# A linear-attention and rational-MLP kernel on one core: a new order of the steps behind step 107

## The chip, the core and the metric

One core of a Trainium2 chip. The metric is the device time of one execution in microseconds (us). Five instruction streams run beside each other and wait for one another through semaphores: PE (TensorE), DVE (VectorE), ACT (ScalarE), POOL (GpSimd) and SP (SyncE, here only an issuer of DMAs). Each works through its own instructions strictly in the order in which they were written.

## The reference

Gated linear attention over 4 batches, 8 heads, 768 positions and 48 channels, followed by a two-layer MLP with a rational activation on all 3072 tokens:

```
f = sigmoid(f_logit)                                   # per batch, head, position, channel
state_t = f_t * state_(t-1) + k_t v_t^T                # 48x48 per head
y_t = q_t state_t                                      # 8 heads x 48 = 384 per token
h = y @ w_in                                           # 384 -> 2048
P = a0 + a1 h + a2 h^2 + a3 h^3
Q = 1 + |b0| |h| + |b1| h^2
out = (P / (Q + 1e-6)) @ w_out                         # 2048 -> 384
```

## The kernel before

The tokens are cut into 12 units of 256 tokens: unit n is chunk n // 4 of batch n % 4, so four units of one chunk are independent and unit n needs the state that unit n - 4 left. Everything that a unit needs is cut into small steps, and one long string, `ORDER` (line 19), names all 823 steps of the 12 units in the order in which they are recorded. A step is a function of the same name (table `steps`, line 587); it writes one instruction or several dozen, all on one engine. `ORDER` therefore fixes the order of every engine's instructions and of every DMA queue. No scheduler moves anything afterwards; semaphores only make an instruction wait until its inputs are there and its buffer is free. The first number of a step is its unit, the last two, where there are any, the blocks of 128 hidden channels (0 to 16) that it covers, and `@s` names one of four PSUM slots that a tile takes.

The steps that the text below speaks of:

- loads: `ld n f|k|q` on SP, `ld n v` on POOL (both line 193); `wi`, `wo` load the weights on POOL (lines 199, 205).
- attention: `ef`, `ls` (ACT, sigmoid in logs), `cs` (PE, prefix sums), `A` (ACT, exponentials), `xa n 0|1` (DVE, scaled q and k, line 308), `T` (PE transposes), `Te` (ACT copy), `sc` (PE scores), `mk` (DVE mask, line 353), `vm n 0|1` (POOL, two small copies of V columns, line 360), `yb`, `yi` (PE, outputs, line 367), `kv`, `si` (PE), `ae` (ACT) and `st` (DVE, line 445) for the state, `ye` (ACT copy to `xT`).
- MLP: `h` (PE, 12 matmuls for 4 blocks, line 454), `hy` (ACT cast to bf16, line 484), `sq` = h^2 (DVE, line 489), `ab` = |h| (DVE, line 497), `p1`, `pm`, `p2` (DVE, lines 531, 545, 536) for P; the sum that ends P is made either by DVE (`tv`, line 553) or by an accumulating DMA that POOL issues (`ta`, line 549); likewise the sum in Q by DVE (`zv`, line 515), by a POOL DMA (`zd`, line 519) or on PE (`u`, line 505). `lz` or `ln` takes the logarithm of Q (ACT, lines 523, 510), `ex` its negative exponential (ACT, line 527), `gm` multiplies (DVE, line 557), `o` is the second matmul (PE, line 567), `oe` the copy out (line 574), `so` the store. `dz` is a dummy matmul (line 295).

The V columns of a unit go to one of two buffers, `vmp0` for even units and `vmp1` for odd ones. Two of the steps on POOL, one DVE step and the loop that records the steps read:

```python
def vm(n, x):
    s = unit(n)
    vv = s["v"].rearrange("p (a r) i d -> p r i a d", r=2)
    src = vv[:, 0, :, :, 32:48] if x == 0 else vv[:, 1, :, :, 0:16]
    nc.gpsimd.tensor_copy(s["vm"][:, :, :, 32 * x:32 * x + 16], src)
def ta(n, m0, m1):
    nc.gpsimd.dma_start(out=fl(s["g"], m0, m1), in_=fl(s["hy"], m0, m1), accum_op=ALU.add)
def gm(n, m0, m1):
    return nc.vector.tensor_mul(fl(s["g"], m0, m1), fl(s["g"], m0, m1), fl(qi, m0, m1))
for step in ORDER.replace("\n", ";").split(";"):
    name, *args = step.split()
    marks[...] = steps[name](...)
```

Of the kernel before, what the change touches and what calls it, by code (L numbers as in the profile page):

```python
# [32 lines left out]
u 0 8 12 @3; A 3 0; ta 0 8 16; sq 0 0 4; Te 2 s; h 1 0 4 @2; vm 2 1; xa 3 0; wo 8 12; ln 0 8 12; p2 0 0 8
sc 2 0 @0; kv 2 @1; ef 5; mk 2 0; si 2 0; ae 2; hy 1 0 4; sc 2 1 @3; st 2 0; yb 2 0 2 @0; ex 0 8 16; mk 2 1
si 2 1; u 0 0 4 @2; ab 1 0 8; u 0 4 8 @3; ln 0 0 4; st 2 1; p1 1 0 16; u 1 12 16 @1; ln 0 4 8; yi 2 1; sq 1 0 8
ln 1 12 16; yb 2 2 4; kv 3 @3; ye 2 s; pm 1 8 16; T 3 @2; ae 3; ef 4; si 3 0; h 2 0 4 @0; p2 1 0 16; Te 3 s
ls 4; st 3 0; u 1 8 12 @1; ta 1 8 16; pm 0 0 8; hy 2 0 4; ld 7 f; si 3 1; wo 12 16; dz 1 @2; h 2 8 12 @2
ln 1 8 12; st 3 1; ld 5 v; pm 1 0 8; ex 0 0 8; vm 4 1; sc 3 1 @0; sc 3 0 @3; mk 3 1; h 2 4 8 @1; vm 3 1; wo 4 8
hy 2 8 12; wo 0 4; mk 3 0; cs 4 @0; ls 5; vm 4 0; h 2 12 16 @2; vm 3 0; tv 0 0 8; A 4 0; ld 8 f; ld 5 q; A 4 1
xa 4 0; yi 3 1 @3; ld 6 k; yb 3 0 2; hy 2 4 8; ld 6 q; u 1 4 8 @0; xa 4 1; hy 2 12 16; yb 3 2 4; gm 0 8 16  # L40
cs 5 @1; ld 6 v; ye 3 s; T 4 @2; gm 0 0 8; A 5 0; ln 1 4 8; h 3 0 4 @3; p1 2 0 16; Te 4 s; h 3 12 16 @0
ab 2 0 16; hy 3 0 4; o 0 1 8 12 @2; tv 1 0 8; A 5 1; kv 4 @3; hy 3 12 16; sq 2 0 16; u 1 0 4 @1; ae 4; ex 1 8 16
o 0 0 8 12; si 4 0; o 0 1 12 16; xa 5 1; vm 5 1; ln 1 0 4; h 3 8 12 @0; zd 2 8 16; p2 2 0 16; ld 8 k; ef 6
h 3 4 8 @1; ef 7; pm 2 0 16; hy 3 8 12; o 0 1 4 8; hy 3 4 8; sc 4 1 @0; o 0 1 0 4; ls 6; mk 4 1; ta 2 8 16
sc 4 0 @1; ex 1 0 8; o 0 0 0 4; ld 9 f; xa 5 0; cs 6 @0; mk 4 0; o 0 0 4 8; A 6 1; o 0 0 12 16; st 4 0; A 6 0
yb 4 0 2 @1; ab 3 0 16; yb 4 2 4; oe 0 0 2 s; yi 4 0; yi 4 1; si 4 1; sq 3 0 16; ye 4 s; T 5 @2; ef 8
u 2 0 4 @1; Te 5 s; h 4 4 8 @0; st 4 1; zd 3 8 16; ln 2 0 4; gm 1 8 16; h 4 12 16 @2; lz 2 8 16; p1 3 0 16
# [578 lines left out]
```

## Time and profile before

| | us |
|---|---|
| median of 3 runs | 217.37 (215.85 to 218.01) |
| span of the profiled execution, first to last instruction | 214.4 |
| PE busy | 201.0 (94%) |
| DVE busy | 201.7 (94%) |
| ACT busy | 195.8 (91%) |
| POOL busy | 83.7 (39%) |

The span is the only time that the profile gives for the profiled execution; it lies 3.0 us below the median of the runs and 1.45 us below the lowest. What is predicted is the time of such a run. Busy time is time with an instruction in work; DMA issues on POOL count, on SP they don't. Times inside the trace are counted from the start of the span.

### The profile page before, as it was taken

What the parts mean: (1) busy time and instruction counts of PE and PEld (TensorE: products, weight loads), DVE (VectorE), ACT (ScalarE), POOL (GpSimd) and SP (SyncE); (2) the same over time, 40 slices, a digit from 0 to 9 for tenths busy, and PEclk for the clock granted to TensorE, in tenths of its full rate; (3) what the DMA queues carried; (4) which work ended last, traced back from release to release, by engine and by line L of the source; (5) the groups of instructions that cost most, each with busy time, mean ns of one, the idle gap of its engine ahead of it and who ended that gap; (6) DMA issues with size and microseconds to landing.
All of it is one profiled execution on the core that took longest, in us unless ns stands there. A gap on an engine that the chain in (4) does not pass through costs nothing.

```text
span 214.4 us, 7128 instructions
## 1 busy us (share of the span) xinstructions
PE 201.0 (94%) x3166; PEld 139.9 (65%) x3166; DVE 201.7 (94%) x213; ACT 195.8 (91%) x204; POOL 83.7 (39%) x93
## 2 busy tenths in 40 slices
PE   5875999899999999999999899999999999999993
PEld 1544587567767686586687587686577676776461
DVE  4786899999999999999999999999999999999991
ACT  3574689999999999999999999999999999999990
POOL 5161009009165072183270496696350603114200
PEclk9999999999999999999999999999999999999999
DMA  5999999999999999999999499999499896988823
GB/s 143 240 257 217 201 242 197 195 223 223 187 200 248 247 235 219 253 228 203 192 292 193 81 294 215 209 225 208 89 192 200 164 196 126 174 282 151 187 84 148
DMA packets 61199, 43.20 MB, mean 202 GB/s; under 512 B 51184, under 2 KB 55024, under 8 KB 61168
## 3 DMA queue, kind: packets, MB, share of 16 engines
q0 software_dynamic: 21520, 23.86, 67.3%
q1 hardware_dynamic: 39360, 18.68, 34.5%
q8 instruction: 25, 0.41, 0.8%
q10 hardware_dynamic: 288, 0.20, 0.3%
q14 instruction: 6, 0.05, 0.1%
HBM read 25.17 MB, written 4.72 MB: 139 GB/s over the span
## 4 chain that ended last, share of the span: by engine, by line
PE 39%; DVE 29%; ACT 14%; DMA 9%; issue 6%; SPq 2%; POOL 1%; DVEq 0%
PE hp L454 13%; PE op L567 12%; DVE gall L557 6%; DMA w_in_sb<-in_moe_w_in_dram 6%; DVE gall L545 4%; ACT qi L527 4%; ACT hy L484 4%; DVE z L497 3%; DVE h L489 3%; DVE scm L353 3%; DMA fn<-in_f_logit_dram 3%; PE u L505 3%; DVE gall L531 3%; PE y L367 2%; DVE hy L536 2%
## 5 line engine op out<-in xcount | busy, mean ns | idle before, releaser
L567 PE MATMUL op<-w_out_sb,gall 128*128 128x384 bf16 x384 | 69.2, 326 | 0.4 <-DVE gall L557 0.4
L454 PE MATMUL hp<-xT,w_in_sb 128*128 128x256 bf16 x564 | 66.7, 273 | 2.1 <-DMA w_in_sb<-in_moe_w_in_dram 2.0
L454 PEld LDWEIGHTS <-w_in_sb 128*128 128x128 bf16 x564 | 54.2, 98 | 11.5 <-DMA w_in_sb<-in_moe_w_in_dram 2.5
L567 PEld LDWEIGHTS <-gall 128*128 128x128 bf16 x384 | 36.1, 98 | 23.6 <-DVE gall L557 0.8
L484 ACT CAST hy<-hp 128x1024 bf16<-128x1024 f32 x47 | 48.1, 1076 | 2.3 <-PE hp L478 1.4
L527 ACT ACTIVATE qi<-lq 128x2048 bf16<-128x2048 f32 (+1 forms) x26 | 48.0, 1861 | 0.1
L360 POOL COPY vmp<-vn 128x128 bf16<-128x128 bf16 x24 | 35.2, 1516 | 28.4 <-DMA vn<-in_v_dram 22.7
L549 POOL DMA_DIRECT2D gall<-hy x20 | 20.0, 1068 | 53.9 <-ACT lsp L276 10.6
L523 ACT ACTIVATE lq<-z 128x2048 f32<-128x2048 bf16 (+1 forms) x20 | 36.8, 1874 | 0.0
L353 DVE TENSOR_TENSOR scm<-sc,mask 128x1024 bf16<-128x1024 f32 x24 | 29.0, 1215 | 1.9 <-PE sc L345 1.7
L489 DVE TENSOR_TENSOR h<-hy 128x4096 bf16<-128x4096 bf16 (+2 forms) x19 | 28.5, 1500 | 0.0
L557 DVE TENSOR_TENSOR gall<-gall,qi 128x4096 bf16<-128x4096 bf16 (+2 forms) x17 | 28.2, 1666 | 0.2
L545 DVE TENSOR_TENSOR gall<-gall,h 128x4096 bf16<-128x4096 bf16 (+2 forms) x17 | 28.1, 1652 | 0.0
L519 POOL DMA_DIRECT2D z<-h x17 | 19.3, 1366 | 17.0 <-PE u L505 6.0
L302 ACT ACTIVATE A<-cs 128x768 f32<-128x768 f32 (+1 forms) x26 | 19.4, 799 | 1.8 <-PE cs L286 1.8
L193 POOL DMA_DIRECT2D vn<-in_v_dram x12 | 12.4, 1030 | 15.7 <-PE y L367 7.9
L531 DVE TENSOR_SCALAR gall<-hy,a_sb 128x4096 bf16<-128x4096 bf16 (+1 forms) x14 | 16.9, 1208 | 0.0
L536 DVE TENSOR_SCALAR hy<-hy,a_sb 128x4096 bf16<-128x4096 bf16 (+1 forms) x14 | 16.6, 1185 | 0.0
L497 DVE TENSOR_SCALAR z<-hy 128x4096 uint16<-128x4096 uint16 (+2 forms) x19 | 15.7, 834 | 0.4 <-ACT hy L484 0.4
L330 ACT COPY qkT<-tp 128x1024 f32<-128x1024 f32 x11 | 11.6, 1058 | 3.2 <-PE tp L320 3.2
L320 PE MATMUL tp<-ident,qkp 128*128 128x128 bf16 x192 | 12.9, 219 | 0.8 <-DVE qkp L308 0.5
L320 PEld LDWEIGHTS <-qkp 128*128 128x128 bf16 x192 | 11.5, 98 | 2.5 <-DVE qkp L308 0.9
(73 smaller groups left out, 255.8 us busy)
## 6 DMA issues: line engine op xcount, KB each, us to landing
gall<-hy POOLq DMA_DIRECT2D x18, 512.0 KB, 7.1
z<-h POOLq DMA_DIRECT2D x15, 512.0 KB, 8.4
fn<-in_f_logit_dram SPq DMA_DIRECT2D x11, 384.0 KB, 8.5
kn<-in_k_dram SPq DMA_DIRECT2D x11, 384.0 KB, 12.1
qn<-in_q_dram SPq DMA_DIRECT2D x11, 384.0 KB, 11.3
out_dram<-osb SPq DMA_DIRECT2D x11, 384.0 KB, 5.1
vn<-in_v_dram POOLq DMA_DIRECT2D x12, 192.0 KB, 8.9
w_in_sb<-in_moe_w_in_dram POOLq DMA_DIRECT2D x4, 384.0 KB, 10.1
```

Of the source, the lines that this page charges most:

```text
L320: nc.tensor.transpose(t[:, x, i, p, :], s["qk"][:, i, x, 2 * p:2 * p + 2, :].rearrange("t h d -> t (h d)"), ident)
L353: return nc.vector.tensor_mul(t, s["sc", g].rearrange("s r a i t -> s (r a) (i t)"), mb)
L360: nc.gpsimd.tensor_copy(s["vm"][:, :, :, 32 * x:32 * x + 16], src)
L454: nc.tensor.matmul(t[:, m - m0, :], w_in_sb[:, kk, m * P:(m + 1) * P], s["x"][:, kk].rearrange("p i j t -> p (i j t)"), start=(kk == 0), s ...
L484: (nc.scalar.copy if eng == "s" else nc.vector.tensor_copy)(fl(big(s, "hy", "hy", 3), m0, m1), fl(s["hp", m0], 0, m1 - m0))
L489: return nc.vector.tensor_mul(fl(big(s, "h2", "h2", 2), m0, m1), fl(s["hy"], m0, m1), fl(s["hy"], m0, m1))
L523: nc.scalar.activation(fl(lq, m0, m1), fl(s["z"], m0, m1), AF.Ln, scale=regs[2], bias=1.0 + 1e-6)
L527: nc.scalar.activation(fl(qi, m0, m1), fl(lq, m0, m1), AF.Exp, scale=-1.0)
L531: return nc.vector.tensor_scalar(fl(big(s, "g", "gall", 3), m0, m1), fl(s["hy"], m0, m1), a_sb[:, 3:4], a_sb[:, 2:3], op0=ALU.mult, op1=AL ...
L545: return nc.vector.tensor_mul(fl(s["g"], m0, m1), fl(s["g"], m0, m1), fl(s["h2"], m0, m1))
L557: return nc.vector.tensor_mul(fl(s["g"], m0, m1), fl(s["g"], m0, m1), fl(qi, m0, m1))
L567: nc.tensor.matmul(s["op", j][:, j, 0:DM], s["g"][:, m, P * j:P * j + P], w_out_sb[:, m, :], start=(s["on", j] == 1), stop=(s["on", j] == KF))
```

## The change

Only the string `ORDER` changes. Its first 107 steps (up to `A 2 0`) stay as they are. Behind them stand the same 716 steps, each as often as before and with the same arguments, in another order, and some of their PSUM tiles take another of the four slots. No function, shape, buffer or step is added or removed. The changed kernel is one line shorter, so every line number in it is one lower.

```diff
-yb 1 0 2 @1; st 1 0; yb 1 2 4; sq 0 12 16; yi 1 1; si 1 1; p1 0 8 16; ye 1 s; h 0 4 8 @2; ab 0 12 16; ef 3
+yb 1 0 2 @0; vm 2 0; yb 1 2 4; ef 3; st 1 0; sq 0 12 16; p1 0 8 16; yi 1 1; si 1 1; vm 2 1; ye 1 s; h 0 4 8 @1
...
```

Three places show what that does to the queues. On DVE, first, the stretch from the second half of unit 0's P to the first mask of unit 2 (`h2`, which the profile calls `h`, is made by `sq`, `z` by `ab`, `gall` by `p1` and `pm`, `hy` by `p2`, `qkp` by `xa`, `scm` by `mk`); tiles with 467 are unit 0's `hy`, those with 721 or 723 unit 1's. Before:

```order
L536 TENSOR_SCALAR hy_467<-hy_467,a_sb_104 128x2048
L497 TENSOR_SCALAR z_472<-hy_467 128x1024
L489 TENSOR_TENSOR h2_532<-hy_467 128x1024
L308 TENSOR_TENSOR qkp0_87<-kn_326,A_89 128x2x8x48
L497 TENSOR_SCALAR z_740<-hy_721 128x2048
L489 TENSOR_TENSOR h2_760<-hy_721 128x2048
L497 TENSOR_SCALAR z_472<-hy_467 128x1024
L308 TENSOR_TENSOR qkp0_87<-qn_336,A_89 128x2x8x48
L531 TENSOR_SCALAR gall_671<-hy_467,a_sb_104 128x2048
L308 TENSOR_TENSOR qkp1_88<-kn_338,A_89 128x2x8x48
L489 TENSOR_TENSOR h2_532<-hy_467 128x1024
```

and with the change:

```order
L488 TENSOR_TENSOR h2_532<-hy_467 128x1024
L535 TENSOR_SCALAR hy_467<-hy_467,a_sb_104 128x2048
L496 TENSOR_SCALAR z_472<-hy_467 128x1024
L307 TENSOR_TENSOR qkp0_87<-kn_326,A_89 128x2x8x48
L496 TENSOR_SCALAR z_760<-hy_723 128x2048
L488 TENSOR_TENSOR h2_762<-hy_723 128x2048
L307 TENSOR_TENSOR qkp0_87<-qn_336,A_89 128x2x8x48
L488 TENSOR_TENSOR h2_532<-hy_467 128x1024
L530 TENSOR_SCALAR gall_660<-hy_467,a_sb_104 128x2048
L307 TENSOR_TENSOR qkp1_88<-kn_338,A_89 128x2x8x48
L496 TENSOR_SCALAR z_472<-hy_467 128x1024
```

The square `sq 0 4 8` now stands ahead of `p2 0 8 16`, and `ab 0 0 4` and `sq 0 0 4` have changed places across three other steps.

On POOL, second, the same time: the copies `vm` (`vmp<-vn`), the V loads (`vn`; 445 is unit 2's), the weight loads and the first accumulating DMA, `ta 0 8 16` (`gall<-hy_467`). Before:

```order
L360 COPY vmp0_94<-vn_445 128x8x16
L193 DMA vn_779<-in_v_dram 128x8x96
L193 DMA vn_800<-in_v_dram 128x8x96
L549 DMA gall_671<-hy_467 128x2048
L360 COPY vmp0_94<-vn_445 128x8x16
L205 DMA w_out_sb_111<-in_moe_w_out_dram 128x4x384
L549 DMA gall_964<-hy_721 128x2048
```

and with the change, where `vn_791` is unit 3's V and `vn_904` unit 4's:

```order
L359 COPY vmp0_94<-vn_445 128x8x16 x2
L192 DMA vn_791<-in_v_dram 128x8x96
L192 DMA vn_904<-in_v_dram 128x8x96
L204 DMA w_out_sb_111<-in_moe_w_out_dram 128x4x384
L359 COPY vmp0_94<-vn_904 128x8x16
L359 COPY vmp1_95<-vn_791 128x8x16
L548 DMA gall_660<-hy_467 128x2048
```

`ta 0 8 16` has moved behind the copies `vm 4 0` and `vm 3 0`, which read the two V tiles whose loads are issued just ahead.

On POOL, third, the middle of the program: `z` is written by `zd`, `gall` by `ta`. Before (unit 7's V is `vn_1762`; `z_1985` and `gall_2007` are unit 4's):

```order
L360 COPY vmp1_95<-vn_1762 128x8x16
L549 DMA gall_1705<-hy_1371 128x2048
L519 DMA z_1985<-h2_1897 128x2048
L193 DMA vn_2138<-in_v_dram 128x8x96
L193 DMA vn_2322<-in_v_dram 128x8x96
L360 COPY vmp1_95<-vn_1762 128x8x16
L519 DMA z_2243<-h2_2283 128x2048
L549 DMA gall_2007<-hy_1738 128x2048
```

and with the change (unit 8's V is `vn_1832`, unit 7's `vn_2061`; `z_1968` and `gall_2083` are unit 4's):

```order
L192 DMA vn_2061<-in_v_dram 128x8x96
L359 COPY vmp0_94<-vn_1832 128x8x16
L518 DMA z_1968<-h2_1850 128x2048
L359 COPY vmp1_95<-vn_2061 128x8x16
L548 DMA gall_2083<-hy_1704 128x2048
```

`zd 4 8 16` now stands behind the copy `vm 8 1`, which may overwrite `vmp0` only when `yb 6` has read it, and `ta 4 0 8` behind `vm 7 1`.

More of the change, by code (lines that the diff above doesn't have):

```diff
@@ L33 @@
[L33 to L47, printed above, removed]
@@ new lines @@
+h 1 12 16 @0; ls 3; pm 0 8 16; ab 0 12 16; st 1 1; hy 0 4 8; h 1 8 12 @2; sq 0 4 8; hy 1 12 16; hy 1 8 12
+cs 3 @3; p2 0 8 16; ab 0 4 8; h 0 0 4 @0; xa 2 1; h 1 4 8 @2; ab 1 8 16; sq 1 8 16; A 3 1; hy 0 0 4; xa 2 0
+u 0 12 16 @0; T 2 @1; hy 1 4 8; A 3 0; ld 3 v; u 0 8 12 @2; sq 0 0 4; ln 0 12 16; Te 2 s; p1 0 0 8; xa 3 1
+ab 0 0 4; h 1 0 4 @3; sc 2 0 @0; ln 0 8 12; xa 3 0; p2 0 0 8; hy 1 0 4; kv 2 @1; si 2 0; dz 1 @2; sc 2 1 @3
+mk 2 0; ae 2; ld 4 v; st 2 0; mk 2 1; ex 0 8 16; yb 2 0 2 @0; si 2 1; st 2 1; u 0 0 4 @2; ef 5; ln 0 0 4
@@ new lines @@
+ef 7; sc 4 0 @1; mk 4 0; cs 6 @0; o 0 0 8 12; o 0 0 4 8; xa 5 0; yi 4 1 @1; yi 4 0; yb 4 0 2; ld 7 k; A 6 1
+yb 4 2 4; oe 0 0 2 s; si 4 1; T 5 @2; A 6 0; ab 3 0 16; sq 3 0 16; ye 4 s; ta 2 0 8; st 4 1; u 2 0 4 @1
+h 4 4 8 @0; lz 2 8 16; p1 3 0 16; gm 1 8 16; gm 1 0 8; Te 5 s; h 4 0 4 @3; hy 4 4 8; ln 2 0 4; h 4 12 16 @2
+ef 8; h 4 8 12 @0; sc 5 0 @1; pm 3 0 16; hy 4 12 16; zd 3 8 16; hy 4 0 4; u 2 4 8 @2; ta 2 8 16; hy 4 8 12
+sc 5 1 @3; mk 5 0; ex 2 8 16; kv 5 @0; ld 6 v; si 5 0; zd 3 0 8; ae 5; vm 5 1; mk 5 1; ld 8 v; o 1 1 12 16 @1
@@ new lines @@
+pm 4 0 16; o 2 1 8 12; p2 4 0 16; o 2 1 4 8; o 2 0 4 8; o 2 1 12 16; st 6 0; ld 10 f; ld 8 k; ex 3 0 8; mk 6 0
+xa 7 1; hy 5 12 16; ex 3 8 16; o 2 1 0 4; yi 6 0 @0; yi 6 1; ls 8; T 7 @1; so 0 0 2 s; lz 4 0 8; o 2 0 8 12
+si 6 1; Te 7 s; tv 4 8 16; sq 5 0 16; yb 6 0 2; yb 6 2 4; ye 6 s; o 2 0 0 4; ab 5 0 16; oe 2 0 2 s; vm 8 1
+cs 8 @1; ld 8 q; st 6 1; h 6 0 4 @0; ld 11 f; ld 9 k; zd 4 8 16; vm 7 1; ta 4 0 8; A 8 0; A 8 1; vm 7 0
+sc 7 1 @2; gm 3 0 16; h 6 4 8 @3; hy 6 0 4; ef 10; ld 9 q; h 6 12 16 @0; o 3 1 12 16 @1; vm 8 0; so 2 0 2 s
@@ new lines @@
+mk 7 1; p1 5 0 16; sc 7 0 @2; zd 5 0 8; hy 6 4 8; kv 7 @3; ex 4 0 8; xa 8 1; hy 6 12 16; si 7 0; o 3 1 8 12
+zv 5 8 16; o 3 1 0 4; ae 7; ld 9 v; ld 10 q; mk 7 0; h 6 8 12 @0; yb 7 2 4 @2; yb 7 0 2; lz 4 8 16; st 7 0
+yi 7 1; si 7 1; p2 5 0 16; xa 8 0; ls 9; hy 6 8 12; pm 5 0 16; o 3 0 8 12; ta 5 8 16; ld 10 v; o 3 0 12 16
+cs 9 @0; yi 7 0; st 7 1; o 3 0 0 4; ex 4 8 16; gm 4 0 16; A 9 1; ye 7 s; o 3 0 4 8; o 3 1 4 8; A 9 0; lz 5 8 16
+ab 6 0 16; sq 6 0 16; h 7 8 12 @3; h 7 4 8 @0; oe 3 0 2 s; kv 8 @2; hy 7 8 12; ef 11; si 8 0; T 8 @1; ae 8
@@ new lines @@
+hy 7 4 8; xa 9 1; Te 8 s; h 7 0 4 @3; hy 7 0 4; st 8 0; sc 8 0 @2; kv 9 @0; p1 6 0 16; ld 10 k; vm 9 0; ta 5 0 8
+zd 6 8 16; sc 8 1 @3; zd 6 0 8; vm 9 1; o 4 1 8 12 @1; o 4 0 12 16; mk 8 0; mk 8 1; si 9 0; o 4 0 8 12
+h 7 12 16 @2; ls 10; ex 5 8 16; lz 5 0 8; pm 6 0 16; yi 8 0 @3; yb 8 0 2; ae 9; st 9 0; yb 8 2 4; o 4 0 4 8
+vm 10 1; yi 8 1; o 4 1 4 8; xa 9 0; p2 6 0 16; ls 11; hy 7 12 16; ex 5 0 8; o 4 1 12 16; cs 10 @0; ye 8 s
+o 4 0 0 4; o 4 1 0 4; T 9 @2; h 8 0 4 @3; A 10 0; A 10 1; oe 4 0 2 s; h 8 8 12 @1; sq 7 0 16; lz 6 8 16
@@ new lines @@
+o 5 1 4 8; o 5 0 8 12; si 10 0; dz 3 @2; h 9 0 4 @2; p1 8 0 16; h 9 8 12 @3; lz 7 0 8; ta 7 0 8; ae 10; st 10 0
+oe 5 0 2 s; p2 8 0 16; ex 7 0 8; zd 8 8 16; hy 9 0 4; hy 9 8 12; lz 7 8 16; h 9 4 8 @1; xa 11 1; xa 11 0
+sc 10 1 @2; sc 10 0 @0; h 9 12 16 @3; hy 9 12 16; hy 9 4 8; mk 10 1; ex 7 8 16; mk 10 0; o 6 1 8 12 @2
+o 6 1 4 8; o 6 1 12 16; T 11 @0; yi 10 0 @3; yi 10 1; ta 7 8 16; yb 10 2 4; yb 10 0 2; Te 11 s; so 3 0 2 s
+o 6 0 8 12; pm 8 0 16; o 6 0 4 8; ab 9 0 16; sc 11 0 @1; sq 9 0 16; mk 11 0; o 6 0 0 4; o 6 0 12 16; ta 8 8 16
@@ new lines @@
+o 6 1 0 4; ye 10 s; lz 8 0 8; lz 8 8 16; h 10 0 4 @1; gm 7 0 16; oe 6 0 2 s; h 10 8 12 @3; ta 8 0 8; hy 10 0 4
+sc 11 1 @2; h 10 12 16 @1; p1 9 0 16; ex 8 0 8; kv 11 @0; hy 10 8 12; ex 8 8 16; mk 11 1; ae 11; p2 9 0 16
+o 7 0 4 8 @2; pm 9 0 16; hy 10 12 16; o 7 1 8 12; h 10 4 8 @3; si 11 0; o 7 0 8 12; gm 8 0 16; zd 9 0 8
+hy 10 4 8; o 7 1 0 4; o 7 1 4 8; yi 11 0 @3; lz 9 0 8; st 11 0; so 1 0 2 s; o 7 0 12 16; yi 11 1; yb 11 0 2
+yb 11 2 4; sq 10 0 16; zd 9 8 16; o 7 1 12 16; o 7 0 0 4; lz 9 8 16; ab 10 0 16; p1 10 0 16; zv 10 0 8; ye 11 s
@@ new lines @@
+h 11 8 12 @1; o 8 0 8 12 @0; ex 9 0 8; hy 11 8 12; oe 7 0 2 s; ta 9 8 16; ex 9 8 16; o 8 0 4 8; ta 9 0 8
+o 8 0 12 16; p2 10 0 16; o 8 1 0 4; h 11 0 4 @3; h 11 12 16 @2; zd 10 8 16; o 8 0 0 4; pm 10 0 16; o 8 1 12 16
+o 8 1 4 8; o 8 1 8 12; ab 11 8 12; gm 9 0 16; sq 11 8 12; lz 10 0 8; so 7 0 2 s; lz 10 8 16; hy 11 12 16
+o 9 1 12 16 @1; h 11 4 8 @2; ex 10 8 16; ex 10 0 8; tv 10 8 16; p1 11 8 16; oe 8 0 2 s; o 9 0 0 4; o 9 1 0 4
+sq 11 12 16; ab 11 12 16; pm 11 8 12; o 9 1 8 12; o 9 0 8 12; o 9 1 4 8; ta 10 0 8; p2 11 8 16; gm 10 0 16
@@ new lines @@
+pm 11 12 16; so 6 0 2 s; hy 11 0 4; o 9 0 4 8; o 9 0 12 16; so 8 0 2 s; zd 11 8 12; hy 11 4 8; lz 11 8 12
+sq 11 0 4; sq 11 4 8; ab 11 4 8; ab 11 0 4; o 10 0 0 4 @0; oe 9 0 2 s; o 10 0 12 16; so 9 0 2 s; o 10 1 12 16
+zd 11 12 16; ta 11 8 12; o 10 1 8 12; p1 11 0 8; lz 11 12 16; ex 11 8 12; o 10 0 8 12; ex 11 12 16; so 5 0 2 s
+u 11 4 8 @1; ln 11 4 8; p2 11 0 8; ta 11 12 16; zv 11 0 4; ex 11 4 8; lz 11 0 4; pm 11 0 4; o 10 1 0 4
+o 10 1 4 8; o 10 0 4 8; ex 11 0 4; gm 11 12 16; o 11 0 12 16 @1; pm 11 4 8; gm 11 8 12; o 11 1 12 16 @3
@@ L98 @@
+o 11 0 8 12; oe 10 0 2 s; so 10 0 2 s; tv 11 4 8; o 11 1 8 12; gm 11 4 8; o 11 0 4 8; o 11 1 4 8; tv 11 0 4
+gm 11 0 4; o 11 1 0 4; o 11 0 0 4; dz 1 @2; oe 11 0 1 v; oe 11 1 2 s; so 11 0 1 s; so 11 1 2 a
 """
```

73 lines of the change are left out of this document (20 added, 53 removed).

## The prediction

> **What bounds the kernel now.** I read the page first, for which engine is full, then the table of windows, for where it is full, then the waits, and last the chain of waits, for what sets the end.
>
> ```profile
> span 214.4 us, 7128 instructions
> PE 201.0 (94%) x3166; PEld 139.9 (65%) x3166; DVE 201.7 (94%) x213; ACT 195.8 (91%) x204; POOL 83.7 (39%) x93
> DVE  4786899999999999999999999999999999999991
> PE 39%; DVE 29%; ACT 14%; DMA 9%; issue 6%; SPq 2%; POOL 1%; DVEq 0%
> ```
>
> Three engines are busy for over 90% of the span, so no single share names the bound. The tenths of DVE do: after the first slices it never drops below 9 until the last one. The windows (PE, PEld, DVE, ACT, POOL in this order) put numbers to it:
>
> ```profile
> core 0: us, PE busy (x) PEld busy (x) DVE busy (x) ACT busy (x) POOL busy (x), PEclk, DMA share, GB/s
> 16.00:36.00 20.00, 16.80 (x281) 13.22 (x282) 17.01 (x26) 13.96 (x17) 4.96 (x8) 1.00 1.20 217
> 36.00:209.20 173.20, 170.65 (x2681) 119.65 (x2680) 172.84 (x151) 172.44 (x172) 71.36 (x67) 1.00 1.02 200
> ...
> DVE osb L574 <- PE op L567: 1.2, 1, 1.2
> ```
>
> From 36.0 to 209.2 us DVE works 172.84 of 173.20 us: 0.36 us idle in 151 instructions. Its only recorded wait behind 36 us (the last row, from the waits of that stretch) is the final copy, which waits for the last matmuls. ACT is idle for 0.76 us in the same stretch, PE for 2.55. The granted clock is 1.00. So the middle is a chain of DVE instructions, with ACT and PE hardly behind.
>
> The end is PE's, as the chain of waits shows (start, length, what):
>
> ```profile
> 197.18 2.21 DVE gall L557
> 199.44 2.12 PE op L567 x12
> 201.56 0.86 PE u L505 x4
> 202.42 8.46 PE op L567 x52
> 210.91 0.48 ACT osb L574
> ```
>
> When `gm 10 0 16` is done, 64 matmuls of `o 10` and `o 11` and one `u` are left: 2.12 + 0.86 + 8.46 = 11.4 us without a gap, then a copy and a store.
>
> **The change part by part.** The steps are the same, so each engine has the same work, and with DVE 99.8% busy from 36 us on the order cannot shorten that stretch by more than its 0.36 us of idle time plus whatever instructions were stretched. I therefore look for three things: DVE waits that go, DVE waits that come, and the end.
>
> *Early, on DVE: 0 to 0.5 us gained, I take 0.2.*
>
> ```profile
> 30.68 0.95 DVE L308 TENSOR_TENSOR qkp<-kn,A 128x768 bf16<-128x768 f32 x1
> 31.98 0.69 DVE L497 TENSOR_SCALAR z<-hy 128x2048 uint16<-128x2048 uint16 x1 [0.35 <-ACT hy L484]
> 33.72 0.52 DVE L497 TENSOR_SCALAR z<-hy 128x1024 uint16<-128x1024 uint16 x1
> 35.02 1.15 DVE L531 TENSOR_SCALAR gall<-hy,a_sb 128x2048 bf16<-128x2048 bf16 x1
> 36.95 0.77 DVE L489 TENSOR_TENSOR h<-hy 128x1024 bf16<-128x1024 bf16 x1
> 38.52 0.80 DVE L536 TENSOR_SCALAR hy<-hy,a_sb 128x2048 bf16<-128x2048 bf16 x1
> 39.24 1.21 DVE L353 TENSOR_TENSOR scm<-sc,mask 128x1024 bf16<-128x1024 f32 x1
> ...
> 30.93 1.01 ACT L484 CAST hy<-hp 128x1024 bf16<-128x1024 f32 x1 [0.30 <-PE hp L454]
> ...
> 38.03 0.42 PE L345 MATMUL sc<-qkT 48*64 48x128 bf16 x16
> ```
>
> `sq 0 4 8`, moved ahead of `p2 0 8 16`, now comes about 0.3 us before its `hy 0 4 8` is cast. But DVE waits anyway until 31.98 for `hy 1 8 12` (the ACT row), which comes from the third `h` in both orders; the new wait eats the 0.35 us of the old one. From 31.98 to the first mask the instructions are the same and took 7.26 us. Three were slow: the 35.02 row took 1.15 us where a similar one (38.52) took 0.80, the 33.72 and 36.95 rows 0.1 over the usual. Without these 0.54 us the mask would start at 38.7, and its scores (38.03 + 0.42) are there. What slowed them? All three lie beside POOL's work, which is only rearranged:
>
> ```profile
> 32.68 1.28 POOL L360 COPY vmp<-vn 128x128 bf16<-128x128 bf16 x1 [8.01 <-DMA vn<-in_v_dram]
> 33.91 1.75 POOL L193 DMA_DIRECT2D vn<-in_v_dram  x2
> 35.64 0.97 POOL L549 DMA_DIRECT2D gall<-hy  x1
> 36.29 0.89 POOL L360 COPY vmp<-vn 128x128 bf16<-128x128 bf16 x1
> 37.13 0.76 POOL L205 DMA_DIRECT2D w_out_sb<-in_moe_w_out_dram  x1
> 48.48 0.86 POOL L549 DMA_DIRECT2D gall<-hy  x1 [10.60 <-ACT lsp L276]
> ...
> DMA to landing us min/median/max: 7.4/9.5/11.6
> ...
> vn<-in_v_dram POOLq DMA_DIRECT2D x12, 192.0 KB, 8.9
> ...
> 56.27 2.36 DVE L557 TENSOR_TENSOR gall<-gall,qi 128x2048 bf16<-128x2048 bf16 x2
> ```
>
> So I count less than half of it.
>
> *`ta 0 8 16` behind two copies: 0 to 3.9 us lost, I take 0.* Before, it was issued at 35.64, took the 11.6 us of the landing row (the 7.4 are `ta 1 8 16`, issued at 48.48) and was down at 47.2, 9 us ahead of `gm 0 8 16` at 56.27. Now the V load of unit 4 leaves about 0.9 us later (the second `vm 2` copy stands ahead), at some 35.7; with the page's 8.9 us or a little more it is down at about 45.4. Then `vm 4 0`, `vm 3 0` (0.3 to 1.3 us each), and `ta 0 8 16` is issued between 46 and 48. With 7.4 us, as its neighbour needed at that time of the program, it lands at 53.5 to 55.4; `gm 0 8 16` has the same DVE work ahead of it as before and wants it at 56.27 less the early gain, 55.7 to 56.3. Nine microseconds of cover have become 0.3 to 2.8. With 11.6 us it is down at 57.7 to 59.6, and DVE loses 1.4 to 3.9 us. I take the landing row of the neighbour: w_out's first load is then the only POOL transfer ahead.
>
> *The middle, `zd 4 8 16` and `ta 4 0 8` behind `vm 8 1` and `vm 7 1`: 0 to 0.7 us lost on DVE, I take 0.3.*
>
> ```profile
> 104.79 0.25 PE L367 MATMUL y<-scm,vn 64*32 64x128 bf16 x4
> ...
> 115.06 2.03 ACT L523 ACTIVATE lq<-z 128x2048 f32<-128x2048 bf16 x1
> ...
> 124.94 2.28 DVE L557 TENSOR_TENSOR gall<-gall,qi 128x4096 bf16<-128x4096 bf16 x1
> ...
> DMA to landing us min/median/max: 8.5/8.5/8.5
> DMA to landing us min/median/max: 9.9/9.9/9.9
> L360 POOL COPY vmp<-vn x3: 295/296/5924, 121.4 to 127.5; 128x128 bf16<-128x128 bf16 x3
> ```
>
> `vm 8 1` must wait for `yb 6` (its last matmuls: 104.79 + 0.25; one `o` of 0.65 us more stands ahead now: 105.7). It then needs 0.3 us, or until DVE's next pause: 106.0 to 107.5. `zd 4 8 16` took 8.5 us, so z lands at 114.5 to 116.0. `lz 4 8 16` ran at 115.06 and has one ACT step of 0.73 us (`ef 11`) less ahead: it wants z at 114.3. ACT waits 0.2 to 1.7 us. `gm 4 0 16` ran at 124.94; `ab 6`, `sq 6` and `xa 9 1` (1.13 + 2.20 + 0.87 = 4.2 us from start to start) now follow it, so it wants its `ex 4 8 16` at 120.7, which without the wait ends at 119.7. One microsecond of ACT's wait is covered, 0 to 0.7 reach DVE. `ta 4 0 8` (9.9 us) follows one copy later, at 107 to 110.8: down at 117 to 120.7, just in time.
>
> *The end: 0.1 us lost.* The last matmuls are now those of the half that DVE copies (0.56 us, against ACT's 0.48). PE's 11.4 us behind `gm 10` stay. PE was ready for them only 0.4 us before `gm 10` ended, so of any gain on DVE no more than 0.4 us would arrive.
>
> *Elsewhere* the steps that a DVE instruction reads from ACT or PE stand as far ahead of it as before: counted in work between them, the tightest pairs (`ex` ahead of `gm 6`, `gm 8`, `gm 10`; `sc` ahead of `mk`) keep 0.8 us or more. SP's loads, f, q and k of units 5 to 11, change places among themselves; I found none moved close to its user.
>
> **Sum:** -0.2 + 0 + 0.3 + 0.1 = +0.2 us on a span of 214.4. I add the 3.0 us by which the median of the runs lies above it and forecast **217.5 us**, no change. The bounds of these terms are -0.3 (0.4 of the gain arrives, the end costs 0.1) and +4.7 (3.9 + 0.7 + 0.1).
>
> **Rivals.**
>
> 1. *Slower: `ta 0 8 16` lands late.* For it: its cover falls from 9 us to 0.3 to 2.8, and the other landing of the pair was 11.6. Against: that one had two V loads just ahead. Price, when it takes 11.6 us and 0.2 is gained: 1.6 to 3.5 us straight on DVE (wanted at 56.1), 219.1 to 221.0. It decides from a landing over 8 to 10 us after the issue. Chance 0.17.
>
> 2. *Slower: one copy blocks POOL.* The same `vm` copy took 295 ns and 5924 ns (the row above, around 121 to 127 us), while DVE ran without a pause. If `vm 8 1` needs 5.9 us, `zd 4 8 16` starts at 111.6, z lands at 120.1, ACT waits 5.8 us, of which 1.0 is covered: DVE loses 4.8 us, 222. Of three copies in that row one was so slow; here a state update of DVE comes within 2 us, which is why I give it 0.05. The Trainium skill, "SBUF — State Buffer", section "Who interferes with whom", has a rule for this: DVE and GpSimd share a port pair that one instruction locks for its whole length, and a DVE instruction with at most one SBUF input and outside the 2-port modes leaves it free. The 5924 ns, which ended under a state update (one input in PSUM), agree with that. By the rule `vm 8 1` is let in under `st 6 1` at the latest, so the sum would stay as it is; and POOL, where it starts first, may hold DVE up in turn, of which the rows above show 0.54 us.
>
> 3. *ACT falls behind for good.* ACT has 0.76 us of idle time from 36 us on. If it waits the full 1.7 us for z, it stays late, and DVE pays 1.3 us more at the next places where `ex` is just in time: 218.5 to 219. Chance 0.15.
>
> 4. *Faster: the runs, not the order.* The three runs lie 2.2 us apart. If what makes the median 1.5 us longer than the lowest is transfers that come late, an order with more room where it matters would pull the median down to 215.9, and with the capped 0.4 us to 215.5. Against: at the places above the new order has less room, not more. Chance 0.18, of which 0.1 passes the 1% bound (below 215.2).
>
> **How the numbers follow.** The forecast and its surroundings (216.3 to 218.4) keep 0.45. Differences under 1% are about what a measurement of this kernel can't tell from no change. Over 1% slower (above 219.5) are rival 2 and most of rival 1: 0.20. Over 1% faster: 0.10. The rest, 0.70, is no change. The range reaches from 215.3 to 220.2 and leaves out about 0.1 on each side.
>
> **What the changed profile would show.** Right: DVE again at 99% or more from 36 us on; `gm` of unit 0 behind `tv` without idle time; the first mask at 38.7 to 39.2; a wait of ACT of 0.2 to 1.7 us at `lq<-z` near 114; about 11.4 us of PE behind the `gm` of unit 10. Wrong: a DVE wait for the DMA `gall<-hy` near 56 (rival 1), a `vmp` copy of several us near 106 (rival 2), DVE waits for ACT's `qi` from 120 us on (rival 3), or a span well under 213.5, which would mean that DVE's instructions themselves became shorter.

## The result and the profile after

| | before | after |
|---|---|---|
| median, us | 216.63 (215.85 to 218.01, 4 runs) | 226.01 (225.59 to 227.24, 4 runs) |
| span of the profiled execution, us | 214.4 | 223.8 |

A ratio, here and below, leaves out the runs that took over 1.5% longer than the fastest of the same kernel (two with 33 extra matmuls, one with 24 and one in experiment 7); the medians keep them.

The changed kernel is **slower: ratio 1.044, 95% interval 1.039 to 1.049**. The forecast was 217.5 us, no change, with a range up to 220.2; the time lies 5.8 us above the range. None of the four rivals was what happened.

The page of the changed kernel, the lines that answer to those of before (PEclk, new here, is the granted clock of PE in tenths, in 40 slices of 5.6 us):

```profile
span 223.8 us, 7123 instructions
PE 202.8 (91%) x3166; PEld 140.1 (63%) x3166; DVE 202.4 (90%) x213; ACT 195.7 (87%) x204; POOL 78.6 (35%) x93
DVE  4886999999999990698999999999999999999981
PEclk9999999999999999679999999999999999999999
```

Every engine has the work it had before, within 2 us but for POOL. The span is 9.4 us longer, and the row of DVE shows at a glance where: one hole, the 16th and 17th slice (a 0 and a 6), and in the 17th and 18th PE's clock was at 6 and 7 tenths. The table of windows around that place (columns as in the table of before):

```profile
36.00:82.70 46.70, 45.93 (x819) 32.47 (x818) 46.70 (x44) 46.70 (x53) 22.18 (x21) 1.00 1.12 203
82.70:91.40 8.70, 3.97 (x52) 2.22 (x52) 1.21 (x2) 6.07 (x6) 0.55 (x2) 0.99 1.27 198
91.40:110.00 18.60, 15.78 (x224) 10.77 (x224) 17.75 (x15) 12.10 (x14) 3.76 (x5) 0.82 0.91 171
110.00:218.00 108.00, 106.25 (x1585) 73.98 (x1583) 106.94 (x92) 107.23 (x100) 39.51 (x40) 1.00 0.91 187
```

Up to 82.7 us DVE is busy for 46.70 of 46.70 us. Then it works 1.21 of 8.70. Behind that it is full again but for 0.85 us in the third window and 1.06 in the fourth. What it waited for is in DVE's own timeline, and in the chain of waits (the last row):

```profile
81.56 2.34 DVE L352 TENSOR_TENSOR scm<-sc,mask 128x1024 bf16<-128x1024 f32 x2
91.41 2.29 DVE L488 TENSOR_TENSOR h<-hy 128x4096 bf16<-128x4096 bf16 x1 [7.50 <-DMA z<-h]
...
78.72 12.56 DMA z<-h
```

Before, the same square began without a wait, and the same transfer took 9.1 us:

```profile
85.05 2.27 DVE L489 TENSOR_TENSOR h<-hy 128x4096 bf16<-128x4096 bf16 x1
...
DMA to landing us min/median/max: 9.1/9.1/9.1
```

The waiting instruction is `sq 4 0 16`, the square of unit 4. The DMA is `zd 3 0 8`, the sum in Q of unit **3**: issued at 78.72, down at 91.28. A square of unit 4 needs nothing of unit 3. It waits because it *overwrites* what that transfer reads. The squares (`h2`, called `h` in the profile) lie in a pool of two buffers; a square gets one of them when the program is built, and the addresses in the two built programs say which unit got which:

```
unit           0 1 2 3 4 5 6 7 8 9 10 11
before         A B A B A B A B A B A  B
after          A B A B B A B A B A B  A
```

Before, unit 4 takes the buffer that unit 2 left; after, the one of unit 3, which is still in use. The pools of `z`, `hy` and `gall` hand their buffers out alike in both programs. The two programs' rows of that square name the semaphores accordingly (DMASW are those of POOL's DMA transfers):

```
before  L489 TENSOR_TENSOR h2_1897<-hy_1738 128x4096 [waits DMASW1_49,Activation_49]
after   L488 TENSOR_TENSOR h2_1850<-hy_1704 128x4096 [waits DMASW2_49,DMASW5_49,DVE_49,Activation_49]
```

DMASW2 and DMASW5 are `zd 3 8 16` and `zd 3 0 8`, the two transfers that read unit 3's square. Behind 26 us these are the other waits of ACT, PE and DVE that bear on it:

```profile
ACT A L301 <- PE cs L285: 7.5, 2, 7.2
PE sv L424 <- DVE state L444: 7.4, 1, 7.4
ACT xT L435 <- PE y L366: 1.9, 1, 1.9
DVE scm L352 <- PE sc L344: 0.8, 1, 0.8
DVE gall L556 <- DMA gall<-hy: 0.5, 1, 0.5
```

The first three are the same halt passed on: PE waits 7.42 us for the state update queued behind the square, ACT waits for PE. The 0.8 us is new DVE time, at 103 us: `mk 6 1` waits for scores that come late because PE, after its halt, worked at half its clock. The 0.5 us is at the end.

**Theory A**: the square's buffer is the cause; with it the halt, PE's slow clock and the late scores go. **Theory B**: the new order of transfers is worse by itself (`zd 3 0 8` took 12.56 us here and 9.06 before), and the wait shows up at the square only because it happens to be there.

### The profile page after: what moved, and what is told of

It is laid out like the page before. It is cut to its first block, busy times and chain, and to the rows that moved or that the text cites. A ratio compares the mean times of both kernels' runs of the same rounds, so it can differ in the third digit from the quotient of the medians.

```text
span 223.8 us, 7123 instructions
## 1 busy us (share of the span) xinstructions
PE 202.8 (91%) x3166; PEld 140.1 (63%) x3166; DVE 202.4 (90%) x213; ACT 195.7 (87%) x204; POOL 78.6 (35%) x93
## 4 chain that ended last, share of the span: by engine, by line
PE 34%; DVE 27%; DMA 15%; ACT 12%; issue 8%; SPq 1%; POOL 1%; DVEq 0%; POOLq 0%
PE hp L453 10%; PE op L566 10%; DMA z<-h 6%; DVE h L488 6%; DMA vn<-in_v_dram 4%; DVE gall L556 4%; DVE gall L544 4%; PE y L366 4%; ACT hy L483 3%; DMA fn<-in_f_logit_dram 3%; DVE hy L535 3%; PE u L504 2%; DVE gall L530 2%; DVE scm L352 2%; DVE qkp L307 2%
## 5 line engine op out<-in xcount | busy, mean ns | idle before, releaser
L483 ACT CAST hy<-hp 128x1024 bf16<-128x1024 f32 x47 | 49.0, 1081 | 2.9 <-PE hp L477 1.9
L359 POOL COPY vmp<-vn 128x128 bf16<-128x128 bf16 x24 | 28.5, 1212 | 53.3 <-DMA vn<-in_v_dram 36.0
L518 POOL DMA_DIRECT2D z<-h x17 | 21.4, 1374 | 48.6 <-DMA vn<-in_v_dram 10.9
L301 ACT ACTIVATE A<-cs 128x768 f32<-128x768 f32 (+1 forms) x26 | 20.0, 810 | 9.4 <-PE cs L285 9.3
L192 POOL DMA_DIRECT2D vn<-in_v_dram x12 | 16.2, 1355 | 0.0
L424 PE MATMUL sv<-state,ident 128*128 128x384 bf16 x20 | 6.7, 336 | 7.4 <-DVE state L444 7.4
L270 ACT ACTIVATE fn<-fn 128x768 f32<-128x768 f32 (+1 forms) x13 | 10.9, 838 | 2.8 <-DMA fn<-in_f_logit_dram 2.8
```

The costliest lines, as they stand in the source:

```text
L483: (nc.scalar.copy if eng == "s" else nc.vector.tensor_copy)(fl(big(s, "hy", "hy", 3), m0, m1), fl(s["hp", m0], 0, m1 - m0))
L518: nc.gpsimd.dma_start(out=fl(s["z"], m0, m1), in_=fl(s["h2"], m0, m1), accum_op=ALU.add)
```

## The experiments

The kernel before was run beside each group: 216.51, 216.56 and 216.75 us. Besides the time I compare in the profiled executions the stretch from the first mask of unit 2 (`mk 2 0`) to the last product (`gm 11 0 4`), by their starts on DVE: 169.18 us before, 179.00 after.

**1. The changed order, the two buffers handed out by hand.**

```diff
-big(s, "h2", "h2", 2)
+big(s, "h2", f"h2{n % 2}", 1)
```

> The changed kernel, word for word in its order, with the square's buffer (`h2`) handed out by hand: even units take one, odd units the other. Theory A (the loss is the buffer: the square of unit 4 got the buffer that `zd 3 0 8` was still reading): the 7.50 us wait of `sq 4 0 16` for DMA z<-h goes, the halt of PE of 7.42 us and the low granted clock behind it go too, span 214 to 215.5 us, time 216.0 to 217.5 us, no more than 0.7% from the kernel before. Theory B (the new order of transfers is worse by itself: `zd 3 0 8` and the loads around it land late, whoever holds the buffer): another wait takes the place, at least 220 us. If a rival of the prediction also costs something (late `ta 0 8 16`, ACT behind): 218.5 to 220 us.

217.98 us (216.62 to 219.85, 12 runs), ratio to before 1.0065 (1.0036 to 1.0093). 8.0 of the 9.4 us are gone with a change of addresses only; every engine's instructions stand in the order of the changed kernel. Theory B is out: `zd 3 0 8` took 12.2 us here too, was down at 91.5, and nobody waited for it. The square (first row) and all of DVE's waits behind 26 us:

```profile
84.39 2.27 DVE L488 TENSOR_TENSOR h<-hy 128x4096 bf16<-128x4096 bf16 x1
...
DVE osb L573 <- PE op L566: 1.6, 1, 1.6
DVE gall L556 <- DMA gall<-hy: 0.7, 1, 0.7
DVE state L444 <- PE y L366: 0.5, 1, 0.5
DVE state L444 <- ACT alast L440: 0.2, 1, 0.2
```

The ratio is within the 0.7% that I allowed theory A alone, but the time lies above its 217.5 us and below the 218.5 us at which a rival of the prediction was to show. The stretch takes 170.86 us, 1.7 more than before: 1.5 us are still to be explained.

**2 and 3. One swap on DVE decides the buffer, in both kernels.** `pm 3 0 16` (the product that reads unit 3's square on DVE) and `mk 5 0` stand next to each other in DVE's order. In the changed kernel `pm` is first, before it was second.

```diff
 2: changed kernel
-pm 3 0 16; ... u 2 4 8 @2; ... mk 5 0; ex 2 8 16
+... u 2 4 8 @2; ... mk 5 0; pm 3 0 16; ex 2 8 16
 3: kernel before
-mk 5 0; vm 6 0; u 2 4 8 @2; zd 3 0 8; hy 4 8 12; pm 3 0 16;
+pm 3 0 16; mk 5 0; vm 6 0; u 2 4 8 @2; zd 3 0 8; hy 4 8 12;
```

Experiment 2 has the buffers in turn, A B A B, again; experiment 3 has A B A B B A. No other instruction of any engine moves.

> The changed kernel with one step moved: `pm 3 0 16` behind `mk 5 0` instead of ahead of it, one swap on DVE and nothing on any other engine; the pool then hands the `h2` buffers out in turn again. Theory A: as with the buffers handed out by hand, 216.0 to 217.8 us; `mk 5 0` comes 2.2 us earlier on DVE and may wait for PE by up to 1 us. Theory B: the wait for z<-h stays, since no transfer has moved: 225 to 227 us.

218.75 us (218.52 to 219.78, 4 runs), ratio 1.0114 (1.0076 to 1.0152): the wait for z<-h of DVE is gone. It is above the 217.8 that I gave: `mk 5 0`, now ahead, waits 1.1 us for its scores (the row below), as I had said it might, and the stretch is 171.61 us, 0.75 longer than in experiment 1.

```profile
DVE scm L352 <- PE sc L344: 1.1, 1, 1.1
```

> The kernel before with the opposite swap: `pm 3 0 16` ahead of `mk 5 0` instead of behind it; nothing else moves on any engine, but the pool then gives the square of unit 4 the buffer of unit 3, as in the changed kernel. Theory A: `zd 3 0 8` landed at 89.82 us before and `sq 4 0 16` began at 85.05, so it waits 4.8 to 5.0 us for DMA z<-h; with 0.5 to 1.5 us more behind it (the clock, the next score tile) the span is 219.5 to 221 us, the time 222 to 223.5 us. Theory B (the buffer is harmless, the order of transfers is what costs): 216 to 218 us.

223.62 us (223.31 to 225.94, 4 runs), ratio 1.0364 (1.0313 to 1.0415). The kernel before, with two neighbours exchanged, loses 7.1 us. Its waits:

```profile
DVE h L489 <- DMA z<-h: 4.9, 1, 4.9
PE sv L425 <- DVE state L445: 5.0, 1, 5.0
```

The wait is what the profile of before gives (the transfer down at 89.82, DVE ready for the square at 85.05, 4.8 us); the stretch grew by 6.45 us, so 1.5 us came on top of it, at the upper end of what I expected, and the time lies 0.1 us above my 223.5. This pair shows that the buffer alone does it, in either order of transfers. By which rule the pool picks a buffer is not shown, only that the order of these two steps decides it.

**4. The same buffers, an earlier transfer.**

```diff
-zd 3 8 16; hy 4 0 4; ... ta 2 8 16; ... ld 6 v; si 5 0; zd 3 0 8;
+zd 3 8 16; zd 3 0 8; hy 4 0 4; ... ta 2 8 16; ... ld 6 v; si 5 0;
```

> The changed kernel with `zd 3 0 8` put right behind `zd 3 8 16` on POOL's queue, ahead of `ta 2 8 16` and `ld 6 v`; the `h2` buffers stay as the changed kernel has them (unit 4 in unit 3's). Theory A: the wait of `sq 4 0 16` is the landing of `zd 3 0 8` less its own turn at 82.70 us. Issued near 77.4 instead of 78.72, and with 7.2 to 11 us on the way (its neighbours' 7.16 and 10.77) it lands at 84.6 to 88.5, so the wait is 2 to 6 us instead of 7.50 and the time 220 to 224.5 us. If the price did not hang on this transfer: 225 to 227 us.

221.16 us (220.21 to 222.11, 4 runs), ratio 1.0195 (1.0141 to 1.0250). Issued at 78.17 it took 8.85 us and was down at 87.02; the square waited 2.35 us. DVE was ready for the square at 84.79 (in the changed kernel at 83.91, when its second mask ended, and not at the 82.70 of my expectation, when that mask began). So the wait is the landing less the square's turn on DVE, whatever else stands in the queue.

```profile
87.14 2.29 DVE L488 TENSOR_TENSOR h<-hy 128x4096 bf16<-128x4096 bf16 x1 [2.35 <-DMA z<-h]
```

**5 and 6. PE's halt and its clock.** To see what the slow clock behind the halt costs, PE is kept busy in it with matmuls that nothing reads.

```diff
-o 1 0 4 8; si 5 1; cs 7 @2;
+o 1 0 4 8; dz 33 @2; si 5 1; cs 7 @2;      (then with dz 24)
```

> The changed kernel with 33 matmuls of no use (the same that warm PE at the start) put on PE ahead of `si 5 1`, where it stands still for 7.42 us. The wait of 7.50 us stays in either theory. If the granted clock of 0.6 to 0.7 behind the halt is a result of the halt, it stays at 1 and the 512-wide matmuls of `cs 7` take 0.16 us instead of 0.32: 0.8 to 1.6 us less, 224.4 to 225.2 us. If the clock falls there for another reason, or what follows the halt is not held up by PE: 225.5 to 226.5 us. If the 33 matmuls take longer than the halt: above 226.5 us.

> The changed kernel with 24 matmuls of no use instead of 33 in PE's halt of 7.42 us: 24 took 5.3 us, so that PE still stands for 2 us. If the low clock comes from the length of the halt, `cs 7` runs at 0.16 us each again, as with 33. The time: if the lost clock is on the path, 224.5 to 225.3 us; if DVE and the transfers behind it take the gain back, 225.5 to 226.5 us; if matmuls of no use themselves harm what follows, as the 229.9 us with 33 would have it, above 227 us.

With 33: 229.92 us (226.22 to 231.59, 4 runs), ratio to before 1.052 (1.045 to 1.060, from two runs). With 24: 228.28 us (225.82 to 230.62, 4 runs), ratio to before 1.050 (1.041 to 1.059). The clock did what I expected if the halt is the cause: it stayed at 1. The time did not fall as expected: the 33 end at 94.55 and fill the halt without outlasting it, yet the time is above 226.5; with 24 it is that of the third case, harm to what follows. Windows of the changed kernel, then the same with 24 matmuls (the last three columns are the granted clock, the share of DMA and GB/s):

```profile
90.00:92.00 2.00, 0.00 (x0) 0.00 (x0) 0.59 (x1) 0.00 (x0) 0.00 (x0) 0.80 1.39 190
92.00:94.00 2.00, 0.00 (x0) 0.00 (x0) 2.00 (x2) 0.00 (x0) 0.00 (x0) 0.50 1.23 315
94.00:96.00 2.00, 1.78 (x18) 0.65 (x21) 2.00 (x4) 0.00 (x0) 0.00 (x0) 0.50 0.89 272
96.00:98.00 2.00, 2.00 (x47) 1.14 (x47) 2.00 (x2) 0.81 (x1) 0.34 (x1) 0.50 0.18 49
98.00:100.00 2.00, 2.00 (x24) 1.08 (x23) 2.00 (x3) 1.29 (x2) 2.00 (x5) 0.99 0.51 98
```

```profile
92.00:94.00 2.00, 0.03 (x1) 0.00 (x0) 2.00 (x3) 0.00 (x0) 0.00 (x0) 1.00 1.18 321
94.00:96.00 2.00, 1.94 (x51) 1.12 (x51) 2.00 (x4) 0.81 (x1) 0.00 (x0) 1.00 0.86 262
```

From `si 5 1` to the transposes of unit 6 PE took 5.68 us in the changed kernel (94.22 to 99.90) and 3.99 with the 24 matmuls (94.06 to 98.05): the halved clock costs PE 1.7 us, and `mk 6 1` no longer waits. But the time did not fall. The waits with 24 matmuls say why (ACT's between 82 and 126 us, then two rows of the timelines):

```profile
ACT lq L522 <- DMA z<-h: 3.0, 1, 3.0
...
128.05 0.32 PE L285 MATMUL cs<-lsp,Ui 128*128 128x384 bf16 x1 [2.40 <-ACT hy L483]
...
129.20 0.56 DVE L444 TENSOR_TENSOR state<-sv,alast 128x384 bf16<-128x384 f32 x1 [1.42 <-PE y L366]
```

PE and ACT are ahead by a microsecond, and the store of unit 2 leaves at 114.71 instead of 116.55, now just ahead of `zd 4 8 16` and not behind it. That transfer takes 9.6 us instead of 6.96 (issued 114.81 instead of 115.90, down at 124.43 instead of 122.86), and `lz 4 8 16`, which came just in time at 123.01 in the changed kernel, waits 3.0 us. PE then waits 2.40 us for ACT, and DVE 1.42 us for PE: at `mk 6 1` DVE was 1.07 us ahead of the changed kernel (102.25 against 103.32), at 129.20 it is 0.11 behind. The gain of PE is lost to a transfer with no room. In smaller waits from 142 us on DVE loses 1.8 us more, and their cause is open. That the store is what slowed it is likely from the order of the two, but not shown; nor is why the runs scatter over 5 us with the extra matmuls.

**7 and 8. Where the last 1.5 us are.** On top of experiment 1, first the store `so 5` earlier on SP, so that it does not leave while `ta 11 12 16` is on its way; then also `vm 8 1` out of the way of `zd 4 8 16` on POOL.

```diff
 7
-so 7 0 2 s; lz 10 8 16; ... ex 11 12 16; so 5 0 2 s
+so 7 0 2 s; so 5 0 2 s; lz 10 8 16; ... ex 11 12 16
 8, besides
-vm 8 1; cs 8 @1; ... zd 4 8 16; vm 7 1; ta 4 0 8; ... vm 7 0
+cs 8 @1; ... zd 4 8 16; vm 7 1; ta 4 0 8; ... vm 7 0; vm 8 1
```

> The changed kernel with the `h2` buffers handed out in turn by hand (as in the first experiment, 217.98 us) and the store `so 5` right behind `so 7` on SP, near 188 us, instead of behind `so 9` at 202.7, where `ta 11 12 16` is on its way (4.71 us against 3.25 before) and `gm 11 12 16` waits 0.69 us for it. If the store is what slows that transfer: the wait falls to 0 to 0.2 us, 217.2 to 217.6 us. If not: 217.8 to 218.2 us.

> As the kernel with the early store, and besides `vm 8 1` behind `vm 7 0` on POOL's queue, so that `zd 4 8 16`, `vm 7 1` and `ta 4 0 8` need not wait there for unit 8's copy (106.84 us in the first experiment). If POOL's order in the middle is what holds `st 7 1` and `lz 4 8 16` (0.54 us on DVE): 216.6 to 217.2 us. If PE is what is late there: the same as without it, 217.2 to 217.6 us. If the copy or the transfers now fall on something else: above 218 us.

With the store alone: 217.33 us (12 runs), ratio 1.0028 (1.0001 to 1.0056), by its interval not apart from experiment 1. The time is in the band that I gave for the store as the cause, but by luck, for my reason fails: `ta 11 12 16` still took 4.5 us and `gm 11 12 16` still waits (the row below), so the store was not what slowed it. With both: **216.55 us** (215.85 to 217.46, 12 runs), ratio 0.9996 (0.9970 to 1.0022), the time of the kernel before, and clearly below experiment 1. The stretches are 169.83 and 169.27 us, against 170.86 in experiment 1 and 169.18 before.

```profile
206.03 0.69 DVE L556 TENSOR_TENSOR gall<-gall,qi 128x1024 bf16<-128x1024 bf16 x1 [0.50 <-DMA gall<-hy]
```

Taken together the two moves are worth the 1.5 us; how much belongs to each is not settled.

**9 and 10. The same two moves with the changed kernel's own buffers, without and with 24 matmuls in the halt.**

> The changed kernel with the early store `so 5` and `vm 8 1` behind `vm 7 0`, but with its own `h2` buffers, so that `sq 4 0 16` waits 7.5 us as in the changed kernel. If the three costs simply add (8.0 us for the buffer, 0.65 for the store, 0.78 for the copy), 226.0 - 1.4 = 224.6, between 224.0 and 225.2 us. If the small two cost nothing behind the long wait: 225.6 to 226.4 us.

> The same with 24 matmuls of no use in PE's halt. With POOL's queue in this order `zd 4 8 16` no longer leaves behind `vm 8 1`, so that what the full clock gains (0.9 us on DVE, `mk 6 1` waiting for its scores) is not lost to a late `lz 4 8 16` as it was with 24 and 33 matmuls before. If that was the reason: 0.5 to 1.0 us below the run without them. If the matmuls of no use do harm in another way: at least 1 us above it, with a scatter of several us as before.

226.76 us (225.80 to 227.72, 6 runs) without, 226.04 (224.71 to 227.92, 6 runs) with. The costs do not add: behind the long wait the two moves bring nothing, and in the profiled execution the half clock lasted to 100 us and `mk 6 1` waited 1.5 us instead of 0.8. With the matmuls the clock stays at 1, `lz 4 8 16` does not wait and the median falls by 0.7 us, as expected, but the intervals (1.042 to 1.049 and 1.040 to 1.049 of the kernel before) overlap; `gm 11 12 16` waits 0.9 us for its transfer there. So the clock's price on the time is 0.7 us by the medians; from the two intervals it may be anything from nothing to about 2 us.

## Why the prediction was wrong, point by point

**The step that failed is "*Elsewhere*".** It said that "the steps that a DVE instruction reads from ACT or PE stand as far ahead of it as before", and with that closed the list. It looked at what a DVE instruction reads, and from ACT and PE only. It did not ask what an instruction *overwrites*, who still reads that, and whether the buffer is the same one as before. For the copies `vm`, whose buffers go by name, the prediction did ask it; for the squares it did not. I took for granted that unit n inherits the square of unit n - 2. In the changed program unit 4 inherits that of unit 3, whose last reader is a DMA. The three rivals on the slower side were about values that arrive late; the cause was a buffer that came free late. Both facts stood in the program before any run: the addresses and the semaphores of the row of `sq 4 0 16`. With them the sum was to be had: 89.8 (landing of `zd 3 0 8` before) less 85.1 (turn of the square) is 4.8 us, and already outside my range. Most of the rest of the 7.50 us is the new order's: the transfer came down 1.5 us later (91.28) and DVE was ready 1.1 us earlier (83.91).

**The bound, right.** DVE is the bound: a wait put on it (experiment 3, 4.9 us), taken from it (1, 7.5 us) or shortened (4, by 5.1 us) moves the time by 7.1, 8.0 and 4.8 us, the whole wait or more, but for 0.3 us in the last.

**Early, gain too small to be seen.** The first mask starts at 38.96 instead of 39.24 (predicted 38.7 to 39.2):

```profile
38.96 1.21 DVE L352 TENSOR_TENSOR scm<-sc,mask 128x1024 bf16<-128x1024 f32 x1
...
56.11 1.21 DVE L556 TENSOR_TENSOR gall<-gall,qi 128x2048 bf16<-128x2048 bf16 x1
...
47.82 1.72 POOL L548 DMA_DIRECT2D gall<-hy  x1
...
DMA to landing us min/median/max: 7.8/7.8/7.8
```

But `A 2 0`, the last step that both orders share, already started 0.17 us earlier in that execution (24.98 against 25.15). From there to the mask it is 13.98 us against 14.09: 0.1 gained, not 0.2, and in experiment 1, with the same order, 14.09.

**`ta 0 8 16`, right, and as thin as said.** Issued at 47.82 (predicted 46 to 48), 7.8 us on the way (taken 7.4), down at 55.65; `gm 0 8 16` started at 56.11 without a wait, 0.46 us behind the landing. Rival 1 did not happen, with some luck: `ta 1 8 16`, issued at 51.75, took 16.8 us.

**The middle, right in its steps.** In the changed kernel the long halt hides this place; experiment 1 shows it. `vm 8 1` ran from 106.84 to 107.99 and ended 0.23 us after `st 6 1` began (107.76), let in under that update as the prediction's rival 2 has it; the 5924 ns copy of before ended 0.23 us into a state update too (127.37, begun at 127.14). No `vm` copy near it took 5.9 us, and rival 2 did not happen. `zd 4 8 16` was down at 115.02 (predicted 114.5 to 116.0), and ACT, which came at 115.04, did not wait. DVE lost 0.5 us at `st 7 1` (predicted 0 to 0.7), but to PE and not to ACT.

**The end, size wrong.** With the buffers in turn the new order costs 1.5 us, not the 0.2 of my sum, and the largest piece on record is here. I gave the end 0.1 us for the last copy. `gm 11 12 16` waits 0.5 us for `ta 11 12 16` in the changed kernel, 0.7 in experiment 1; before, the transfer was down in 3.25 us and nobody waited. The later copy itself cost nothing: from `gm 11 0 4` to the end it is 5.97 us in experiment 1, 5.95 before. Experiment 8 has the 1.5 us back; which of its two moves does how much is not settled.

**What lies around the span, too large.** I added 3.0 us to the span. Each profiled execution since has its own time, 1.7 to 1.8 us above its span (223.8 and 225.59; 216.3 and 218.04). The sum itself, 214.4 + 0.2 + 3.0, gives 217.6 and not 217.5.

Without the buffer the forecast of 217.5 stands beside 217.98 in experiment 1, partly by luck: the terms of the order were 1.3 us too small and what lies around the span 1.2 us too large.

## What to carry to other kernels

When an order of steps is changed, a pool can hand the same buffers to other users: compare buffer by buffer which earlier tile each one replaces, and who reads that last, before any duration is weighed. A DMA as last reader is the dangerous case, since it lets go of the buffer late: `zd` transfers of half a unit took 4.8 to 14.0 us from issue to landing in the two kernels. Where two buffers are meant to alternate, giving each its own name keeps them alternating whatever the order of the steps: here that was worth 8 us.

## What the runs showed of the hardware

**PE's clock changes in steps of 3.41 us.** In the changed kernel it fell to 0.50 at 91.21, 4.4 us after the halt of 7.42 us began (at 86.80), and rose at 98.04, 3.8 us after work went on at 94.22. That is 6.83 us at half clock, twice 3.41. In all 12 profiled executions every stretch at half clock that ends before the execution does lasts 3.41 us or two or three times that (10.24 in experiment 9). In one execution the falls lie whole numbers of such steps apart (experiment 3: 22.98 and 94.66, 21 steps). So I laid these steps over each execution and took PE's busy time in each. The 16 steps at full clock behind which the clock fell held 0 to 1.69 us of work; of the 713 behind which it did not fall, two held 1.62 and 1.64, all others 1.72 or more. In these runs, then, the clock falls behind a step in which PE stood still for about half of it, and where a halt lies in the steps counts as much as its length. In experiment 4 a halt of 2.28 us lay within one step, which held 1.14 us of work (first row); in experiment 6 a halt of 2.03 us was divided between two, which held 2.48 and 2.31 (last three rows):

```profile
86.84:90.25 3.41, 1.14 (x8) 0.58 (x6) 3.11 (x3) 2.98 (x2) 0.00 (x0) 1.00 1.29 164
90.25:93.66 3.41, 3.41 (x53) 1.55 (x50) 3.41 (x4) 0.81 (x1) 0.51 (x2) 0.50 1.42 211
93.66:97.08 3.42, 3.42 (x45) 2.53 (x44) 3.42 (x4) 2.81 (x4) 3.42 (x5) 1.00 1.18 321
...
89.55:92.96 3.41, 2.48 (x12) 1.02 (x11) 1.71 (x1) 0.00 (x0) 0.00 (x0) 1.00 1.37 222
92.96:96.37 3.41, 2.31 (x53) 1.22 (x52) 3.41 (x5) 0.81 (x1) 0.00 (x0) 1.00 0.89 272
96.37:99.79 3.42, 3.42 (x45) 2.64 (x45) 3.42 (x4) 2.93 (x5) 2.28 (x5) 1.00 0.32 64
```

The Trainium skill, "TensorE: Matmul & The Clock Gate", Part 1, gives two states, half and full, with an idle or a busy window of some 3.4 us between them. The two states and the length agree with the 0.50 and the 3.41 us. That the window must be idle does not: 1.14 us of work in it did not keep the clock up.

**The same happens near the start, in some executions only.** Between 17 and 27 us, where both orders are alike up to 25 us, the clock stayed at 1.00 in the profiled executions of both kernels and of experiments 1 and 6, and was at half for one step of 3.41 us in all the others. Experiment 8:

```profile
22.00:24.00 2.00, 2.00 (x10) 1.34 (x10) 2.00 (x3) 0.19 (x1) 0.08 (x1) 0.50 1.20 202
24.00:26.00 2.00, 2.00 (x46) 0.96 (x44) 0.74 (x1) 1.63 (x2) 0.45 (x2) 0.67 1.23 204
```

The first mask came at 39.56 to 40.20 there, against 38.96 to 39.52 with the full clock. Such a step shows in the mean clock of a run, by 0.008 (half of 3.41 us in 214.4). Of the 51 runs of the kernel before beside the experiments, the 26 with a mean clock of 0.997 or more have a median of 216.08 us, the 23 with 0.989 to 0.992 one of 216.88. So one step at half clock goes with about 0.8 of the 2.7 us by which these runs differ; where it lay in them is not on record.
